# A hedgehog linear-attention layer and a GEGLU FFN on one core: an eight-bank PSUM pool, and phi_q@KV two tiles at a time

## The chip, the core and the metric

The kernel runs on one NeuronCore of a Trainium2 chip. TensorE multiplies matrices into PSUM (eight banks of 128 partitions by 512 fp32). VectorE and ScalarE read PSUM, do the elementwise work and write SBUF; GpSimd works from SBUF alone; SyncE issues the DMAs. The engines run side by side and wait for each other through semaphores. The metric is the device time of one execution in microseconds.

## The reference

A sequence of 2048 rows of width 640, bf16. First the attention layer on the layer-normed input, 32 heads of width 20, then the FFN on the layer-normed sum:

```
q, k, v = layernorm(x) @ wqkv                       # 2048 x 640 each, 32 heads of 20
phi(a)  = [softmax(a @ w_phi), softmax(-a @ w_phi)]  # per head: 20 + 20 features
kv      = phi(k)^T @ v ; z = sum_s phi(k)            # per head: 40 x 20 and 40
o       = phi(q) @ kv / (phi(q) @ z + 1e-6)
h       = x + o @ wo
out     = h + (gelu(layernorm(h) @ w_gate) * (layernorm(h) @ w_up)) @ w_down   # inner width 1536
```

## The kernel before

The rows are 16 tiles of 128, in four blocks of four tiles. The first part (up to about 90 us) makes the normed input, transposed, in four SBUF tiles LN1T0 to LN1T3; from it k, v and q. It accumulates phi(k)^T v over all 16 tiles in one PSUM tile and masks it into KV (line 352). Exp of q and of -q stay in SBUF, transposed, as Eq (line 367), unnormalised: since the positive and the negative features have their own denominators, the products for each sign s are kept apart.

From line 490 on, PSUM is one pool `psG` of four slots of two banks; every PSUM tile (`gtile`, line 100) takes one. The framework picks the slot and makes the next writer wait until all readers of the slot's former tile have finished. Where a tile has two banks, a reader of one bank waits, as the trace shows, for the products of both.

A tile t of attention output goes through these steps, each a function of its own:

- `attn_a` (522): phi_q@KV. Twenty matmuls of 64 contraction rows by 88 columns, those of the upper and the lower 64 rows (u = 0, 1) into two PSUM tiles `ab`, so that both half-arrays work at once; for each sign s one bank of each. Then two copies of 128x704 fp32 into an SBUF tile AB. In the main part both are ScalarE's; for tiles 0 and 1 one, for tile 2 both are VectorE's.
- `attn_b`, `attn_b2`, `attn_b3` (526 to 558): denominators and weights on GpSimd (`pr`, `den`, `w`), a reciprocal `rd` on VectorE, and on VectorE the weighted numerators `tt` and their sum `o`. Then a DMA transposes o into oT.
- `attn_c` (565): o @ wo, ten matmuls into a two-bank tile `po`.
- `attn_d` (574), `attn_d2` (587): VectorE adds po to x_sb and sums the row on the way; ScalarE sums the squares; five GpSimd ops make the scale and shift of the second layer norm.
- `attn_e` (604): ScalarE applies them (ln), a DMA transposes into LN2T of the tile's block.

The FFN has two kinds of units. `gate_up(b, f, a0, a1)` (610) makes 128 of the 1536 inner features for the columns a0 to a1 of block b: five gate matmuls in one bank, five up matmuls in the other bank of one tile `gu`; Gelu on ScalarE reads the first, a product on VectorE (GT) reads the second and ends the tile's life. `down(b, tl, u)` (623) makes half u (320 columns) of an output tile: twelve matmuls into one bank of `pd`; after both halves VectorE adds x_sb to all 640 columns in one instruction (y, line 641), and a store follows later.

The order of work is written out by hand: a manual schedule fixes each engine's instructions in program order. `weave(units, stages)` (657) walks through a list of units, and before unit i it emits every stage whose number is at most i; what is left goes over to the next weave. `attn_at(t, i, offs)` gives tile t's steps the numbers i + offset.

- Before the weaves: tiles 0 and 1 run between the last q products; then `attn_e(1)` (a transpose on TensorE and a VectorE copy into LN2T), then `attn_a(2, 2)`.
- Weave 1 has 16 units: block 0, columns 0 to 256, twelve gate/up units (0 to 11), then four downs (12 to 15) for its tiles 0 and 1. Beside it run tiles 2 to 6.
- Weave 2 is the same for columns 256 to 512 and tiles 2 and 3, with tile 7 and what is left.
- Then blocks 1 to 3, twelve 512-wide gate/up units and eight downs each. Beside block b run the four tiles of block b + 1.

So `attn_a` comes 14 times in the weaves or just ahead of them, one tile at a time, between units.

Of the kernel before, what the change touches and what calls it, by code (L numbers as in the profile page):

```python
# [8 lines left out]
BF16 = mybir.dt.bfloat16  # L9
F32 = mybir.dt.float32  # L10
ALU = mybir.AluOpType
ACTF = mybir.ActivationFunctionType
AX = mybir.AxisListType
PSUM = bass.MemoryType.PSUM
# [3 lines left out]
def kernel(  # L18
# [12 lines left out]
    nc = tc.nc  # L31
    P = 128
    S = 2048
    D = 640
    H = 32
# [3 lines left out]
    NB = NT // 4  # L39
    NC = D // P  # L40
    NF = FF // P
    EPS = 1e-5
    HD = D // 2
# [15 lines left out]
    KC = Dh + 2  # L59


    UH = H // 2
# [3 lines left out]
    o_v = out.rearrange("b (p t) d -> p (b t) d", t=NT)  # L66
# [25 lines left out]
    def eq(t, c, s):  # L92
        for E, g in zip(Eq, QG):
            if t // 4 * NC + c in g:
                return E[:, g.index(t // 4 * NC + c), s, t % 4 * P:(t % 4 + 1) * P]

    def small(pool, shape, name, bufs=3):
        return pool.tile(shape, F32, name=name, bufs=bufs)

    def gtile(name):  # L100
        return psG.tile([P, 2, 512], F32, name=name, tag="G")
# [49 lines left out]


    mid = ctx.enter_context(tc.tile_pool(name="mid", bufs=1, side="right"))
    LN1T = [mid.tile([P, NC, 512], BF16, name=f"LN1T{b}") for b in range(NB)]
    Wq2 = mid.tile([P, NC, D], BF16, name="Wq2")
    p1_cm = tc.tile_pool(name="p1", bufs=1, reuse_waits="tile")
    p1 = p1_cm.__enter__()
# [329 lines left out]
    ev_cm.__exit__(None, None, None)  # L487
    p1_cm.__exit__(None, None, None)
    ps_cm.close()
    psG = ctx.enter_context(tc.tile_pool(name="psG2", bufs=4, space=PSUM, reuse_waits="tile"))  # L490


    p2 = ctx.enter_context(tc.tile_pool(name="p2", bufs=1, reuse_waits="tile"))
# [1 line left out]
    Wd = p2r.tile([P, NF, D], BF16, name="Wd")  # L495
    nc.sync.dma_start(Wd, B_w_down.rearrange("(c p) n -> p c n", p=P))

    LN2T, st = {}, {}

    def attn_a_mm(t):  # L500

        b = t // 4
        if b not in LN2T:
            LN2T[b] = p2.tile([P, NC, 512], BF16, name="LN2T", bufs=2)
        AB = p2r.tile([P, 2, H, KC], F32, name="AB", bufs=2)
        ab = gtile("ab"), gtile("ab")
        for s in range(2):
            for c in range(NC):
                for u, r in enumerate(HALF):
                    nc.tensor.matmul(ab[u][:, s, 3 * c * KC:(3 * c + 4) * KC], lhsT=eq(t, c, s)[r],  # L510
                                     rhs=KV[r, c, s].rearrange("p h f -> p (h f)"),
                                     start=(c == 0), stop=(c == NC - 1), skip_group_check=True)
        st[t] = AB, ab

    def attn_a_ev(t, dve=0):
        AB, ab = st[t]
        for u in range(2):
            (nc.vector.tensor_copy if u >= 2 - dve else nc.scalar.copy)(  # L518
                AB[:, :, u * UH:(u + 1) * UH].rearrange("p s h f -> p s (h f)"), ab[u][:, :, 0:UH * KC])
        st[t] = AB  # L520

    def attn_a(t, dve=0):
        attn_a_mm(t)
        attn_a_ev(t, dve)

    def attn_b(t, on_pe=False):

# [36 lines left out]

    def attn_c(t):

        po = gtile("po")
        for u in range(2):
            for c in range(NC):
                nc.tensor.matmul(po[:, u, 0:HD], lhsT=st[t][:, c, :], rhs=Wo[:, c, u * HD:(u + 1) * HD],  # L570
                                 start=(c == 0), stop=(c == NC - 1))
        st[t] = po

    def attn_d(t, act=True):

        ht = x_sb[t // 4][:, t % 4, :]
        h2 = ht.rearrange("p (u f) -> p u f", u=2)
        if not act:
            nc.vector.tensor_tensor(h2, st[t][:, :, 0:HD], h2, ALU.add)
            st[t] = ln_stats(p2, [ht], "2", False)[0]  # L580
            return

        sm = small(p2, [P, 2], "sm", 2)
        nc.vector.scalar_tensor_tensor(h2, st[t][:, :, 0:HD], 1.0, h2, op0=ALU.mult, op1=ALU.add, accum_out=sm[:, 0:1])
        st[t] = sm

    def attn_d2(t):
        sm = st[t]
        ht = x_sb[t // 4][:, t % 4, :]
        sq = p2.tile([P, D], BF16, name="sq", bufs=1)  # L590
        nc.scalar.activation(sq, ht, ACTF.Square, accum_out=sm[:, 1:2])
        v = small(p2, [P, 3], "v2", 2)
        nc.gpsimd.tensor_scalar(v[:, 0:1], sm[:, 0:1], sm[:, 0:1], -1.0 / (D * D), op0=ALU.mult, op1=ALU.mult)
        nc.gpsimd.tensor_scalar_add(v[:, 0:1], v[:, 0:1], EPS)
        nc.gpsimd.tensor_scalar(v[:, 1:2], sm[:, 1:2], 1.0 / D, v[:, 0:1], op0=ALU.mult, op1=ALU.add)
        rstd = small(p2, [P, 1], "rstd2")
        nc.gpsimd.tensor_tensor(rstd, v[:, 1:2], nhalf[:, 0:1], op=ALU.pow)
        nc.gpsimd.tensor_scalar(v[:, 2:3], sm[:, 0:1], rstd, -1.0 / D, op0=ALU.mult, op1=ALU.mult)  # L598
        st[t] = ht, None, rstd, v[:, 2:3]
# [8 lines left out]
        transpose_to(LN2T[t // 4][:, :, t % 4 * P:(t % 4 + 1) * P], ln, on_pe, on_dve)  # L608

    def gate_up(b, f, a0, a1):  # L610
        gu = gtile("gu")
        n = a1 - a0
        for i, W in ((0, Wg), (1, Wu)):
            for c in range(NC):
                nc.tensor.matmul(gu[:, i, 0:n], lhsT=W[:, c, f * P:(f + 1) * P], rhs=LN2T[b][:, c, a0:a1],  # L615
                                 start=(c == 0), stop=(c == NC - 1))
        g = p2.tile([P, 512], BF16, name="g", bufs=3)
        nc.scalar.activation(g[:, 0:n], gu[:, 0, 0:n], ACTF.Gelu_apprx_tanh)  # L618
        if (b, "g", f) not in st:
            st[b, "g", f] = p2.tile([P, 512], BF16, name="GT", bufs=NF + 2)  # L620
        nc.vector.tensor_tensor(st[b, "g", f][:, a0:a1], gu[:, 1, 0:n], g[:, 0:n], ALU.mult)  # L621

    def down(b, tl, u):
        if u == 0:
            st["pd"] = gtile("pd"), p2.tile([P, D], BF16, name="y", bufs=4)
        pd, y = st["pd"]
        if u == 1 and b == NB - 1 and tl == 3:
            pd = gtile("pd")
        last = b == NB - 1 and tl == 3

        cuts = [(0, 192), (192, HD)] if last and u == 1 else [(0, HD)]
        for n0, n1 in cuts:
            if n0:
                pd = gtile("pd")
            for f in range(NF):
                nc.tensor.matmul(pd[:, u, n0:n1], lhsT=st[b, "g", f][:, tl * P:(tl + 1) * P],  # L636
                                 rhs=Wd[:, f, u * HD + n0:u * HD + n1], start=(f == 0), stop=(f == NF - 1))
            if u == 1 or last:
                a = u if last else 0
                r = lambda x: x.rearrange("p (u f) -> p u f", u=2)[:, a:u + 1, n0:n1]  # L640
                nc.vector.tensor_tensor(r(y), pd[:, a:u + 1, n0:n1], r(x_sb[b][:, tl, :]), ALU.add)  # L641
                f0, f1 = a * HD + n0, u * HD + n1
                stores.append((lag, o_v[:, 4 * b + tl, f0:f1], y[:, f0:f1]))
                if b == NB - 1 and tl >= 2:
                    store(lag)

# [10 lines left out]
    def weave(units, stages):  # L657

        stages = sorted(later + stages, key=lambda x: x[0])
        later.clear()  # L660
        for i, (fn, *args) in enumerate(units):
            while stages and stages[0][0] <= i:
                _, g, *a = stages.pop(0)
                g(*a)
            store(1)
            fn(*args)
        later.extend((i - len(units), g, *a) for i, g, *a in stages)

    def gus(b, a0, a1):
        return [(gate_up, b, f, a0, a1) for f in range(NF)]  # L670

    def downs(b, tls):
        return [(down, b, tl, u) for tl in tls for u in range(2)]


    q_mm(q)
    attn_a(0, 1)
    q_exp(q)
    q_mm(q + 1)
    attn_b(0, True)  # L680
    attn_b2(0, True)
    attn_b3(0, True)
    attn_a(1, 1)
    q_exp(q + 1)
    q_mm(q + 2)
    attn_t(0)
# [21 lines left out]
        q_exp(j)  # L708
    attn_ln(1, True)
    attn_e(1, True, True)  # L710
    attn_a(2, 2)
    assert q + 9 == len(Eq)

    def attn_at(t, i, offs):

        fns = (attn_a, attn_b, attn_b2, attn_b3, attn_c, attn_d, attn_d2, attn_e)
        return [(i + o, fn, t) for fn, o in zip(fns, offs) if o >= 0]

    SHORT = (0, 2, 3, 4, 9, 9, 10, 12)
    SHORT2 = (0, 2, 3, 4, 10, 10, 11, 13)  # L720
    LONG = (0, 1, 2, 3, 6, 6, 7, 8)


    weave(gus(0, 0, 256) + downs(0, (0, 1)),
          attn_at(2, 0, (-1, 0, 1, 2, 7, 7, 8, 10)) + attn_at(3, 1, SHORT) + attn_at(4, 6, SHORT2) + attn_at(5, 9, SHORT2) +
          attn_at(6, 13, SHORT2))
    weave(gus(0, 256, 512) + downs(0, (2, 3)), attn_at(7, 0, SHORT))
    for b in range(1, NB):
        stages = []
        if b + 1 < NB:  # L730
            for tl in range(4):
                stages += attn_at(4 * b + 4 + tl, (0, 2, 5, 7)[tl], LONG)
        weave(gus(b, 0, 512) + downs(b, range(4)), stages)
    man_cm.__exit__(None, None, None)


# [28 lines left out]
```

## Time and profile before

| | us |
|---|---|
| median of three runs (278.71 to 279.73) | 279.65 |
| span of the profiled execution, first to last instruction | 277.2 |
| outside that span (median less span) | 2.45 |
| TensorE busy | 271.6 (98%) |
| VectorE busy | 167.3 (60%) |
| ScalarE busy | 143.5 (52%) |
| GpSimd busy | 94.7 (34%) |
| first gate product starts at | 90.88 |
| block 0 of the FFN ends, block 1 begins | about 141.4 |
| granted TensorE clock, all of the span | 1.0 |

The profiler lists instructions with start and duration on one core; PE is TensorE, DVE VectorE, ACT ScalarE, POOL GpSimd. Matmuls are pipelined: a matmul's duration is longer than its distance to the next one. In a timeline line the columns are start, time from the first start to the last end, engine, line, operation, output and inputs, shapes, count, and in brackets the idle time before it with what ended it. The chain that ended last is followed back from the last instruction; its columns are start, time, engine, what, count. VectorE is busiest early: its busy share is nine tenths and more in the slices up to 76 us, some six tenths between 91 and 141 us (31.25 of 50.40), and a half in blocks 1 and 2 (46.50 of 93.90).

### The profile page before, as it was taken

To read this page: it belongs to the slowest core of one execution; us is meant where nothing else is said; L and a number is where in the kernel's file an instruction comes from. 1 tells how busy PE (TensorE), PEld (TensorE's weight loads), DVE (VectorE), ACT (ScalarE), POOL (GpSimd) and SP (SyncE) were. 2 spreads that over 40 slices of the span, in tenths; PEclk is the share of its full clock that TensorE was granted. 3 is DMA by queue.
4 is the path that set the end of the run, shared out by engine and by line. 5 is a ranking of instruction groups with operands and counts; after the bars stand their busy time and mean duration, and the time that the engine had idled before them with its cause. 6 is when DMAs were issued, how large, how long until landed. Compare 5 with 4: busy or idle time off the path is not lost.

```text
span 277.2 us, 5817 instructions
## 1 busy us (share of the span) xinstructions
PE 271.6 (98%) x2337; PEld 172.1 (62%) x2337; DVE 167.3 (60%) x292; ACT 143.5 (52%) x239; POOL 94.7 (34%) x213
## 2 busy tenths in 40 slices
PE   7899999999999999999999999999999999999995
PEld 3677777764555887788754555675455567444574
DVE  6799999899496776675325757322666622233222
ACT  4879998778598755374524364413445440222200
POOL 4348997765202217365301353400226230000000
PEclk9999999999999999999999999999999999999999
DMA  7965732489730021324120213130022413000011
GB/s 204 192 232 112 99 74 47 44 256 393 255 102 0 4 47 36 85 49 77 30 65 2 47 27 63 32 88 33 14 36 25 73 25 95 26 0 0 0 50 47
DMA packets 42235, 21.37 MB, mean 77 GB/s; under 512 B 35040, under 2 KB 40416, under 8 KB 42208
## 3 DMA queue, kind: packets, MB, share of 16 engines
q1 hardware_dynamic: 42208, 21.01, 30.8%
q8 instruction: 18, 0.29, 0.5%
q14 instruction: 9, 0.07, 0.1%
HBM read 10.18 MB, written 2.62 MB: 46 GB/s over the span
## 4 chain that ended last, share of the span: by engine, by line
PE 87%; SPq 3%; DMA 3%; DVE 2%; ACT 2%; issue 1%
PE gu L615 38%; PE pd L636 19%; PE pq L362 8%; PE po L570 8%; PE pk L274 5%; PE pv L274 4%; PE ab L510 3%; PE kvp L340 2%; SPq L186 2%; DMA LN1T<-ln 2%; DVE stats L110 1%; DMA WkT<-in_A_wqkv_dram 1%; ACT E L307 1%; ACT ln L134 1%; PE wa L228 1%
## 5 line engine op out<-in xcount | busy, mean ns | idle before, releaser
L621 DVE TENSOR_TENSOR GT<-gu,g 128x512 bf16<-128x512 f32 (+1 forms) x60 | 34.4, 580 | 54.3 <-ACT g L618 54.1
L618 ACT ACTIVATE g<-gu 128x512 bf16<-128x512 f32 (+1 forms) x60 | 30.7, 512 | 69.3 <-PE gu L615 68.5
L615 PE MATMUL gu<-LN2T,Wg 128*128 128x512 bf16 (+1 forms) x300 | 61.9, 337 | 0.1
L615 PE MATMUL gu<-LN2T,Wu 128*128 128x512 bf16 (+1 forms) x300 | 61.8, 337 | 0.0
L636 PE MATMUL pd<-Wd,GT 128*128 128x320 bf16 (+2 forms) x396 | 53.8, 295 | 0.0
L636 PEld LDWEIGHTS <-GT 128*128 128x128 bf16 x396 | 37.9, 98 | 15.3 <-DVE GT L621 0.9
L615 PEld LDWEIGHTS <-Wu 128*128 128x128 bf16 x300 | 29.3, 98 | 22.6
L615 PEld LDWEIGHTS <-Wg 128*128 128x128 bf16 x300 | 28.3, 98 | 20.8
L274 PEld LDWEIGHTS <-LN1T 128*128 128x128 bf16 x290 | 27.9, 98 | 11.0 <-DMA LN1T<-ln 0.3
L322 POOL TENSOR_TENSOR vt<-vS,rs 128x672 bf16<-128x672 bf16 x22 | 29.1, 1344 | 9.1 <-DVE rs L318 7.4
L641 DVE TENSOR_TENSOR y<-pd,x_sb 128x640 bf16<-128x640 f32 (+3 forms) x18 | 13.5, 749 | 30.2 <-PE pd L636 30.2
L518 ACT COPY AB<-ab 128x704 f32<-128x704 f32 x28 | 19.6, 748 | 19.8 <-PE ab L510 19.6
L551 DVE TENSOR_TENSOR tt<-AB,w 128x1280 bf16<-128x1280 f32 x16 | 23.8, 1486 | 1.0 <-POOL w L544 0.9
L570 PE MATMUL po<-Wo,oT 128*128 128x320 bf16 x160 | 24.3, 299 | 0.0
L274 PE MATMUL pk<-Wk,LN1T 128*128 128x320 bf16 x160 | 24.0, 299 | 0.0
L314 DVE TENSOR_REDUCE sk<-E 128x64 f32<-128x1280 bf16 x16 | 22.9, 1434 | 1.2 <-ACT E L307 1.2
L362 PE MATMUL pq<-LN1T,Wq 128*128 128x512 bf16 x100 | 22.9, 379 | 0.0
L367 ACT ACTIVATE Eq<-pq 128x1024 bf16<-128x1024 f32 (+1 forms) x26 | 19.9, 830 | 2.4 <-PE pq L362 2.4
L307 ACT ACTIVATE E<-pk 128x640 bf16<-128x640 f32 x28 | 18.3, 716 | 4.5 <-PE pk L274 4.3
L570 PEld LDWEIGHTS <-oT 128*128 128x128 bf16 x160 | 15.6, 98 | 7.0 <-ACT oT L148 0.3
L274 PE MATMUL pv<-Wv,LN1T 128*128 128x320 bf16 x130 | 19.8, 299 | 0.2 <-DMA LN1T<-ln 0.2
L134 ACT ACTIVATE ln<-x_sb,v,rstd 128x640 bf16<-128x640 bf16 x14 | 12.9, 919 | 11.3 <-POOL v L598 11.1
(101 smaller groups left out, 268.1 us busy)
## 6 DMA issues: line engine op xcount, KB each, us to landing
out_dram<-y SPq DMA_DIRECT2D x15, 160.0 KB, 1.8
Wg<-in_B_w_gate_dram SPq DMA_DIRECT2D x1, 1920.0 KB, 9.4
Wu<-in_B_w_up_dram SPq DMA_DIRECT2D x1, 1920.0 KB, 15.3
Wd<-in_B_w_down_dram SPq DMA_DIRECT2D x1, 1920.0 KB, 7.9
x_sb<-in_A_x_dram SPq DMA_DIRECT2D x2, 640.0 KB, 5.5
Wo<-in_A_wo_dram SPq DMA_DIRECT2D x1, 800.0 KB, 11.1
x_sb<-in_A_x_dram SPq DMA_DIRECT2D x4, 160.0 KB, 3.1
Wv<-in_A_wqkv_dram SPq DMA_DIRECT2D x2, 320.0 KB, 4.1
```

The lines of the kernel that those rows point to most:

```text
L274: nc.tensor.matmul(ps[:, u, 0:HD], lhsT=lnT(t, c), rhs=W[:, c, u * HD:(u + 1) * HD], start=(c == 0), stop=(c == NC - 1))
L307: nc.scalar.activation(Ek[t][:, s, :].rearrange("p (u f) -> p u f", u=2), pk[:, :, 0:HD], ACTF.Exp, scale=((lnp[t][2], nrstd[t]) if t in C ...
L314: nc.vector.reduce_sum(sk, Ek[t].rearrange("p s (h f) -> p (s h) f", f=Dh), axis=AX.X)
L322: eng.tensor_tensor(vt[:, s], vS[t % 8], rs[:, s * H:(s + 1) * H, None].to_broadcast([P, H, VC]), ALU.mult)
L362: nc.tensor.matmul(pqs[j][:, i, :], lhsT=Wq2[:, kc, c * P:(c + 1) * P], rhs=LN1T[b][:, kc, :], start=(kc == 0), stop=(kc == NC - 1))
L367: nc.scalar.activation(Eq[j][:, :, s, :], pqs[j][:, 0:len(QG[j])], ACTF.Exp, scale=(1.0, -1.0)[s])
L551: nc.vector.tensor_tensor(tt.rearrange("p s (h f) -> p s h f", f=Dh), num, w[:, :, :, None].to_broadcast([P, 2, H, Dh]), ALU.mult)
L570: nc.tensor.matmul(po[:, u, 0:HD], lhsT=st[t][:, c, :], rhs=Wo[:, c, u * HD:(u + 1) * HD], start=(c == 0), stop=(c == NC - 1))
L615: nc.tensor.matmul(gu[:, i, 0:n], lhsT=W[:, c, f * P:(f + 1) * P], rhs=LN2T[b][:, c, a0:a1], start=(c == 0), stop=(c == NC - 1))
L618: nc.scalar.activation(g[:, 0:n], gu[:, 0, 0:n], ACTF.Gelu_apprx_tanh)
L621: nc.vector.tensor_tensor(st[b, "g", f][:, a0:a1], gu[:, 1, 0:n], g[:, 0:n], ALU.mult)
L636: nc.tensor.matmul(pd[:, u, n0:n1], lhsT=st[b, "g", f][:, tl * P:(tl + 1) * P], rhs=Wd[:, f, u * HD + n0:u * HD + n1], start=(f == 0), sto ...
```

## The change

From the start of the FFN part, PSUM is a pool `psB` of eight slots of one bank. Gate and up products have a bank each; each half of a down has one and its own VectorE add of 320 columns; po of tiles 2 and up has two banks, with an add and a row sum per bank, and a GpSimd instruction to add the two sums.

`attn_pair(t)` does phi_q@KV of tiles t and t + 1 back to back, forty matmuls into eight banks, and then issues the copies, one for each bank (128x352): the banks of u = 0 on ScalarE, those of u = 1 on VectorE. It is called seven times, for tiles 2, 4, ... 14; the single calls for tiles 3, 4, 5, 6 and 7 stood ahead of units 1, 6, 9 and 13 of weave 1 and unit 0 of weave 2. Pair (2, 3) stands where `attn_a(2, 2)` stood, in the new pool. Pair (4, 5) stands ahead of unit 6 of weave 1, pair (6, 7) ahead of unit 14, pair (8, 9) ahead of unit 14 of weave 2, pair (10, 11) ahead of block 1's first unit, pair (12, 13) ahead of block 1's unit 18 and pair (14, 15) ahead of block 2's first. Five AB tiles are in use instead of two; three of them lie in the memory of LN1T, which therefore becomes one SBUF tile seen in two types. The numbers of the later steps are set anew. In weave 1: tile 2's b3 2, c 7 and e 10; tile 3's b3 at 5 and c at 10 as before; tile 4's b3 at 10; tile 5's b3 at 12 instead of 13. Tile 7's b, b2, b3 and c fall to units 2, 3, 4 and 9 of weave 2.

```diff
-    LN1T = [mid.tile([P, NC, 512], BF16, name=f"LN1T{b}") for b in range(NB)]
+    LN1F = mid.tile([P, NB * NC * 256], F32, name="LN1T")
+    LN1T = [LN1F.bitcast(BF16).rearrange("p (b c n) -> p b c n", b=NB, c=NC)[:, b] for b in range(NB)]
...
+    ABs = [p2r.tile([P, 2, H, KC], F32, name=f"AB{i}") for i in range(2)]
+    ABs += [LN1F[:, i * 2 * H * KC:(i + 1) * 2 * H * KC].rearrange("p (s h f) -> p s h f", s=2, h=H) for i in range(3)]
+    def bank(name):
+        return psB.tile([P, 512], F32, name=name, tag="B")
...
+    def attn_pair(t):
+        for i in (t, t + 1):
+            ab = [[None] * 2, [None] * 2]
+            for s in range(2):
+                for u in range(2):
+                    ab[u][s] = bank("ab")
+            attn_a_mm(i, ab)
+            st[i] = ab
+        for i in (t, t + 1):
+            AB = ABs[i % len(ABs)]
+            for s in range(2):
+                for u, eng in enumerate((nc.scalar.copy, nc.vector.tensor_copy)):
+                    eng(AB[:, s, u * UH:(u + 1) * UH].rearrange("p h f -> p (h f)"), st[i][u][s][:, 0:UH * KC])
+            st[i] = AB
...
-        nc.vector.scalar_tensor_tensor(h2, st[t][:, :, 0:HD], 1.0, h2, op0=ALU.mult, op1=ALU.add, accum_out=sm[:, 0:1])
+        for u in range(2):
+            nc.vector.scalar_tensor_tensor(h2[:, u], st[t][u], 1.0, h2[:, u], op0=ALU.mult, op1=ALU.add,
+                                           accum_out=sm[:, u:u + 1])
...
+        nc.gpsimd.tensor_tensor(sm[:, 0:1], sm[:, 0:1], sm[:, 1:2], ALU.add)
...
-        gu = gtile("gu")
+        gu = bank("gu"), bank("gu")
...
-            if u == 1 or last:
-                nc.vector.tensor_tensor(r(y), pd[:, a:u + 1, n0:n1], r(x_sb[b][:, tl, :]), ALU.add)
+            pd = bank("pd")[:, 0:n1 - n0]
...
+            nc.vector.tensor_tensor(y[:, f0:f1], pd, x_sb[b][:, tl, f0:f1], ALU.add)
...
-    attn_a(2, 2)
+    psB = ctx.enter_context(tc.tile_pool(name="psB", bufs=8, space=PSUM, reuse_waits="tile"))
+    attn_pair(2)
...
+    EARLY = (0, 1, 2, 7, 7, 8, 10)
+    SHORT = (0, 1, 2, 8, 8, 9, 11)
+    LONG = (0, 1, 2, 5, 5, 6, 7)
     weave(gus(0, 0, 256) + downs(0, (0, 1)),
+          attn_at(2, 0, EARLY) + attn_at(3, 3, EARLY) + [(6, attn_pair, 4)] + attn_at(4, 8, SHORT) + attn_at(5, 10, SHORT) +
+          [(14, attn_pair, 6)] + attn_at(6, 15, SHORT) + attn_at(7, 18, EARLY))
+    weave(gus(0, 256, 512) + downs(0, (2, 3)),
+          [(14, attn_pair, 8), (16, attn_pair, 10)] + attn_at(8, 15, LONG) + attn_at(9, 17, LONG) + attn_at(10, 19, LONG) +
+          attn_at(11, 21, LONG))
+    weave(gus(1, 0, 512) + downs(1, range(4)),
+          [(18, attn_pair, 12), (20, attn_pair, 14)] + attn_at(12, 19, LONG) + attn_at(13, 21, LONG) +
+          attn_at(14, 23, LONG) + attn_at(15, 25, LONG))
+    for b in (2, 3):
+        weave(gus(b, 0, 512) + downs(b, range(4)), [])
```

## The prediction

> **What bounds the kernel now.** I read the page's busy times first, then the chain that ended last (in order of time), then the timelines of VectorE, ScalarE and TensorE around the attention products, then the waits.
>
> ```profile
> PE 271.6 (98%) x2337; PEld 172.1 (62%) x2337; DVE 167.3 (60%) x292; ACT 143.5 (52%) x239; POOL 94.7 (34%) x213
> ```
> ```profile
> 90.34 0.50 DVE LN2T L148
> ...
> 90.88 1.25 PE gu L615 x10
> ...
> 188.35 0.50 PE ab L510 x20
> 188.85 4.42 PE gu L615 x20
> ...
> 235.24 25.90 PE gu L615 x120
> ```
> From 32.9 us to the end this chain is TensorE, apart from one 0.5 us eviction at 90.34. In the last block 120 products take 25.90 us, 0.216 each. So whatever TensorE loses or saves after 90 us reaches the end at full price; work of the other engines counts only where TensorE waits for it. The span is 277.2 us, the median 279.65, so 2.45 us lie around the span; I add my sum to the median. About 0.5% (1.4 us) is what a measurement can tell from no change.
>
> ```profile
> 188.28 0.57 PE L510 MATMUL ab<-KV,Eq 64*128 64x88 bf16 x20
> ```
> This TensorE timeline line is one tile's phi_q@KV, "a visit". 0.57 us run from the first start to the last end; one matmul takes 0.20 (its group's mean is 204 ns), so the ten steps (two half-arrays start together) are 0.37/9, or 0.04 us, apart: 0.40 us of streaming. On the chain the visit costs 0.50, and the 20 products behind it take 4.42 instead of 20 x 0.216 = 4.32. So 0.60 per visit, 0.20 of it for going to half-array form and back.
>
> **What the merging saves.** Tiles 0 and 1 are untouched. Of tiles 2 to 15, tile 2's visit (90.23) lies under the LN2T copy that the first gate product waits for, and is free now. Thirteen visits are on the chain: 13 x 0.60 = 7.8 us. Afterwards six pairs cost 2 x 0.40 + 0.20 = 1.00 each: 6.0. The first pair (tiles 2, 3) runs before the FFN, and its eight banks are all of PSUM, so one of them is the bank that the last Exp reads:
>
> ```profile
> 89.47 1.67 ACT L367 ACTIVATE Eq<-pq 128x512 bf16<-128x512 f32 x3
> 91.16 1.28 ACT L618 ACT_TABLE_LOAD   x1
> 92.45 0.38 ACT L618 ACTIVATE g<-gu 128x256 bf16<-128x256 f32 x1
> ```
> That Exp ends at 91.14, and a waiting matmul follows 0.05 later (copy ended 90.83, gate product 90.88). If this bank comes last in the pair, 0.2 of streaming and 0.1 of switch remain: gates start at 91.5, 0.6 later than now. If it comes first: 91.19 + 0.8 + 0.1 = 92.1, 1.2 later. The profile does not show the order of banks; I take +1.0, as most orders block early. Together: -7.8 + 6.0 + 1.0 = -0.8 us (ends -1.2 and -0.6).
>
> The Trainium skill's "TensorEngine Tiling (Array Packing)", Key Properties, says that changing the tiling mode drains TensorE, which is the 0.20 above. Its section on the PSUM bottleneck speaks against this change: tiling speeds up TensorE but not PSUM evacuation. By the first rule alone the sum would end here, at -0.8 us; by the second the waits worked out next come on top, +3.2 in all.
>
> **What the pair waits for.** The copies are issued after both tiles' products, so a pair holds eight banks at once. Its last bank must be the one released last by the work ahead. Today's pool has four units of slack: VectorE may be 2.5 us late and nobody notices. At a pair the slack is gone, except for the 0.1 + 0.6 us until the last quarter is touched.
>
> Pair (4, 5) stands ahead of unit 6, behind six 256-wide gate/up units. VectorE there, today:
>
> ```profile
> 92.87 0.42 DVE L621 TENSOR_TENSOR GT<-gu,g 128x256 bf16<-128x256 f32 x1 [0.35 <-ACT g L618]
> ...
> 94.44 0.42 DVE L621 TENSOR_TENSOR GT<-gu,g 128x256 bf16<-128x256 f32 x1 [0.78 <-ACT g L618]
> 94.78 1.48 DVE L551 TENSOR_TENSOR tt<-AB,w 128x1280 bf16<-128x1280 f32 x1
> ...
> 98.31 1.49 DVE L551 TENSOR_TENSOR tt<-AB,w 128x1280 bf16<-128x1280 f32 x1 [0.32 <-POOL w L544]
> 99.83 0.49 DVE L555 TENSOR_TENSOR o<-tt 128x640 bf16<-128x640 bf16 x1
> 100.24 0.75 DVE L621 TENSOR_TENSOR GT<-gu,g 128x256 bf16<-128x256 f32 x2
> ```
> The sixth GT (unit 5) is the first of the two at 100.24 and ends at 100.66, though its products were done at about 98.2: it is queued behind tile 3's tt and o. The new order keeps that queue (both b3 steps stand ahead of the same units). From the first GT to the end of the sixth is 7.8 us; the 0.78 wait shrinks to about 0.3, as ScalarE has no copies left there: 7.3. The first GT moves: the pair's four ScalarE half-copies now stand between the last Exp and the table load. Gelu at 512 and at 256 elements takes 597 and 383 ns, 0.84 ns an element; a copy of 352 instead of 704 (748 ns) then takes about 450 ns, and some 350 when it follows another (two of 704 together take 1.39 us); four of them, the first ready at about 91.6, end at about 93.0. Load to 94.3, Gelu to 94.7, GT from 94.7, sixth GT done at 102.0. TensorE: gates at 91.9, six units of 1.09, switch 0.1, three quarters 0.6: it wants that bank at 99.1. Stall 2.9. If the load stays ahead of the copies, the first Gelu is set by its products (92.7), GT at 93.1, the sixth done at 100.4: stall 1.2. I take 2.5, nearer the upper end, because the instruction order says so.
>
> Pair (6, 7) stands behind both downs of tile 0. Today those end at 110.82 + 1.63 = 112.45, but the y add runs from 114.35 to 115.16, 2.7 us late, behind tile 5's tt (112.36) and o. If that lateness stays, the pair stalls 2.7 - 0.7 = 2.0; tile 5's b3 now comes one unit (1.63) earlier, which leaves about 0.4, and the add is two of 0.49 in place of one of 0.82. I take 1.0 (0 to 2.0).
>
> Pairs 8 to 14 stand among downs, where VectorE only adds:
>
> ```profile
> 272.68 0.49 DVE L641 TENSOR_TENSOR y<-pd,x_sb 128x320 bf16<-128x320 f32 x1 [0.81 <-PE pd L636]
> ```
> That add starts some 0.2 behind its last product's slot and frees the bank at 0.2 + 0.49 + 0.05 = 0.74, against 0.7: 0.05 each, 0.2 for four (0 to 0.8).
>
> Tile 7's attention chain in the second half of block 0 has the least cover. Today its o ends at 126.32, the transpose lands 2.6 us later (the median of these issues) at 128.9, and its po product starts at 130.15: 1.2 us to spare. The steps from b3 to c stay five units apart. But its b2 step moves behind tile 5's d2 in GpSimd's order (both now fall to the same unit, tile 5 first; today d2 comes a unit later). Today d2 is five small GpSimd ops (with a Square on ScalarE between), which hold its queue for 2.2 us after the po add (tile 6: 130.29 to 132.51); then it is six, 2.5 us. w, and with it VectorE's tt, can be that much later. I take 0.3 us of waiting at po (0 to 1.3: nothing if d2 ends before rd is ready, or 2.5 less the 1.2).
>
> **Costed at nothing.** Splits: the y adds grow by 2 x 0.49 - 0.82 = 0.16 per tile, the po adds by that and a second accumulator read (0.08); VectorE waits 30.2 us for pd in today's run, which covers them outside block 0. Half the AB copies go from ScalarE (748 ns for 704) to VectorE (886; about 0.52 per half, half of 886 and of the 0.16 that a split costs); tile 2's already were there. GpSimd's added 128x1 sum, some 0.27 by the den rows (266 ns), delays each LN2T transpose by that; tile 7's is issued four downs (6.5 us) ahead of its reader, and lands in 2.6. If that cover is gone it costs 0.27 once per block. Gelu waits today for both banks (it starts 0.03 behind the up products); it can now start one bank earlier, which is in my Gelu times. Putting LN1T into one tile costs nothing as long as reuse is tracked by range; the gate products read one half of LN2T unbroken while transposes write the other half.
>
> **Sum.** -0.8 + 2.5 + 1.0 + 0.2 + 0.3 = +3.2 us: 279.65 + 3.2 = 282.85, said as 282.8. The ends add to -1.2 + 1.2 = 0.0 and -0.6 + 2.9 + 2.0 + 0.8 + 1.3 = +6.4, 279.6 to 286.0; all upper ends at once are unlikely.
>
> **Rivals.** (a) VectorE keeps up, and the merging is all that is seen: 279.65 - 0.8 = 278.9, at best 278.4. Place: the sixth GT. It decides if that GT ends by 99.2, and the y add ahead of pair (6, 7) within 0.7. For it speaks the earlier Gelu; against it the 4.0 us of tt and o plus six GTs in line before the bank is freed. This is the not-slower side: no change, 0.13; with one of the switches saved beyond it, faster.
> (b) The lateness spreads: two stalls shift VectorE and GpSimd against each other in block 0, GpSimd's ops stretch beside tt (today v at L593 takes 1436 ns at 107.46 against 264 at rest), oT and LN2T come late, and po products or the last f of a down wait too. A further 1 to 3 us over the sum, 284 to 286: 0.16. Against it: today tiles 4 and 5 have 3.7 us between oT landing and po (tile 4: 111.95 to 115.65).
> (c) The shared LN1T ties transposes in the first stage to readers of other blocks. TensorE has hardly a gap from 33 to 90 us, so any such wait shows: 3 us or more, from 286 on, 0.05. Against it: LN2T above.
> (d) The switch is paid per tile all the same, because a wait falls between the two tiles of a pair: the 7 x 0.20 are lost, +1.2 on the sum, within the range.
>
> **Chances.** Forecast with (d) 0.66, (a) 0.13, (b) 0.16, (c) 0.05. Faster by over 0.5% (below 278.25) needs (a) and more than its best end less 0.15: 0.06. Within 0.5% (to 281.05) takes the rest of (a) and the low end of the forecast: 0.18. Slower 0.76. The range runs from 279.0, just above (a)'s middle, to 285.4, well into (b), and leaves out about 0.2.
>
> **What would show it.** Right: ab in seven runs of 40 with the clock at 1.0; in the pair ahead of unit 6, TensorE idle 2 to 3 us with VectorE GT as releaser, after ten or more ab products; about 1 us at the pair behind tile 0's downs with y as releaser; the first gate product at 91.5 to 92.1; TensorE's waits absent from 140 us on. Wrong: pairs of 1.0 us without a break (rival a), or breaks at po, pd and gu instead of at ab (rival b), or any new gap before 90 us (rival c). The prediction fails most easily in VectorE's lateness at unit 6, since 2.5 of the 3.2 us hang on it.

## The result, and the profile after

The changed kernel takes 283.17 us (median; 282.83 to 284.55) against 279.65 before: a ratio of 1.0148, 95% interval 1.0122 to 1.0174. The profiled execution has a span of 281.5 us with 1.67 around it. For the kernel before, median less span gives 2.45, but other executions of it have about 1.7 around their span (278.98 us against 277.3), so that median and that span are most likely of different executions.

The busy times of the page of after, by engine:

```profile
PE 271.3 (96%) x2324; PEld 173.4 (62%) x2337; DVE 180.9 (64%) x361; ACT 136.9 (49%) x241; POOL 97.3 (35%) x227
```

TensorE is busy for 0.3 us less than before (13 records of matmuls are missing here), in a span 4.3 us longer. The added time is waiting. The chain that ended last (start, length, what), which before was TensorE's from 91 us on, now goes through VectorE, GpSimd and a DMA as well:

```profile
93.72 2.17 issue
...
96.44 1.65 DVE tt L567
...
109.92 1.41 POOL sm L615
...
114.08 1.50 DVE tt L567
...
132.72 2.58 DMA oT<-o
...
265.49 13.08 PE pd L657 x108
```

All but the last of these lie in block 0; behind the DMA it is TensorE's again to the last matmul, apart from pieces of "issue" of 0.05 us ("issue" is time for which the profile shows no cause). TensorE's waits, in its timeline of after, around the first three pairs and at tile 7's po. Each line is a run of matmuls: start, length, then in brackets the idle time ahead of the run and its releaser:

```profile
91.23 1.25 PE L515 MATMUL ab<-KV,Eq 64*128 64x88 bf16 x40 [0.58 <-DVE LN2T L148]
...
99.07 0.60 PE L515 MATMUL ab<-KV,Eq 64*128 64x88 bf16 x21
99.86 0.55 PE L515 MATMUL ab<-KV,Eq 64*128 64x88 bf16 x19 [0.19 <-DVE GT L644]
...
102.53 1.52 PE L590 MATMUL po<-Wo,oT 128*128 128x320 bf16 x10 [0.92 <-DVE GT L644]
...
112.72 1.94 PE L657 MATMUL pd<-Wd,GT 128*128 128x320 bf16 x13 [0.23 <-DVE GT L644]
114.59 0.76 PE L515 MATMUL ab<-KV,Eq 64*128 64x88 bf16 x30
116.55 0.20 PE L515 MATMUL ab<-KV,Eq 64*128 64x88 bf16 x1 [1.20 <-DVE y L659]
116.95 0.35 PE L515 MATMUL ab<-KV,Eq 64*128 64x88 bf16 x9 [0.20 <-DVE y L659]
...
135.35 1.53 PE L590 MATMUL po<-Wo,oT 128*128 128x320 bf16 x10 [0.78 <-DMA oT<-o]
```

The bracket holds idle time only. Below, a "break" is the distance from one matmul's start to the next, less the usual distance for that kind, which also takes in restarting; it is up to 0.2 us more than the bracket.

How to compare two kernels here matters. The time at which the last transpose ahead of the FFN starts lies between 89.73 and 90.72 us in the profiles of the changed kernel and its variants, though nothing ahead of it differs between them. That noise is as large as some of the effects. So I measure the **stretch** from that transpose to the last matmul's start. It is 184.00 us before and 187.91 after: +3.91. Each stretch is read from one profiled execution. The timed ratio gives 1.48% of 279.65, or +4.1.

The parts that can be read from the two traces: from the last transpose to the first gate product 0.80 us before and 1.99 after, +1.19. Break in pair (4, 5) 0.38, at tile 2's po 1.06, in tile 0's downs 0.13 and 0.40, in pair (6, 7) 1.76, at tile 7's po 0.93, at the four late pairs 0.06 each, 0.24: 4.90 together. The merged visits at the working's own prices (6 x 1.00 in place of 13 x 0.60) give -1.8. The sum is 1.19 + 4.90 - 1.8 = +4.29, 0.38 above the 3.91 measured. Of that, 0.25 are three steps of 0.08 in the later downs of the kernel before (at 175.28, 222.16 and 262.55 us), which the changed kernel does not have; the last 0.13 stay open.

### The profile page after: what moved, and what is told of

Same layout as the page of the kernel before. It is cut to its first block, busy times and chain, and to the rows that moved or that the text cites. A ratio compares the mean times of both kernels' runs of the same rounds, so it can differ in the third digit from the quotient of the medians.

```text
span 281.5 us, 5954 instructions
## 1 busy us (share of the span) xinstructions
PE 271.3 (96%) x2324; PEld 173.4 (62%) x2337; DVE 180.9 (64%) x361; ACT 136.9 (49%) x241; POOL 97.3 (35%) x227
## 4 chain that ended last, share of the span: by engine, by line
PE 83%; DVE 4%; SPq 3%; POOL 3%; issue 2%; DMA 2%; ACT 1%; POOLq 0%; DVEq 0%
PE gu L638 32%; PE pd L657 18%; PE pk L275 8%; PE pq L363 7%; PE po L590 7%; PE pv L275 6%; PE kvp L341 2%; PE ab L515 2%; SPq L187 2%; DVE tt L567 2%; DMA WkT<-in_A_wqkv_dram 1%; DMA oT<-o 1%; PE wa L229 1%; DVE LN1T L539 1%; POOL w L560 1%
## 5 line engine op out<-in xcount | busy, mean ns | idle before, releaser
L641 ACT ACTIVATE g<-gu 128x512 bf16<-128x512 f32 (+1 forms) x60 | 30.2, 509 | 77.2 <-PE gu L638 74.6
L638 PEld LDWEIGHTS <-Wg 128*128 128x128 bf16 x300 | 29.0, 98 | 21.3
L659 DVE TENSOR_TENSOR y<-pd,x_sb 128x320 bf16<-128x320 f32 (+2 forms) x33 | 15.8, 481 | 31.0 <-PE pd L657 31.0
L363 PEld LDWEIGHTS <-Wq 128*128 128x128 bf16 x100 | 9.5, 98 | 10.4 <-issue 0.2
L539 ACT COPY LN1T<-ab 128x352 f32<-128x352 f32 x18 | 7.1, 464 | 15.9 <-PE ab L515 15.8
```

What stands on the lines that cost most here:

```text
L363: nc.tensor.matmul(pqs[j][:, i, :], lhsT=Wq2[:, kc, c * P:(c + 1) * P], rhs=LN1T[b][:, kc, :], start=(kc == 0), stop=(kc == NC - 1))
L638: nc.tensor.matmul(gu[i][:, 0:n], lhsT=W[:, c, f * P:(f + 1) * P], rhs=LN2T[b][:, c, a0:a1], start=(c == 0), stop=(c == NC - 1))
L641: nc.scalar.activation(g[:, 0:n], gu[0][:, 0:n], ACTF.Gelu_apprx_tanh)
L659: nc.vector.tensor_tensor(y[:, f0:f1], pd, x_sb[b][:, tl, f0:f1], ALU.add)
```

## The experiments

Each edit is to the changed kernel unless said otherwise. Each ratio is to the kernel before. My theory: four separate places lose the time (the first pair; the sixth GT behind tile 3's b3 step; the y adds of tile 0 behind tile 5's b3; tile 7's b2 behind tile 5's d2 on GpSimd), each by the order of instructions on an engine other than TensorE. Its rivals: the split adds and copies make VectorE too slow for any order; or a wait that is removed only comes up at the next consumer.

**The first pair split.** Tile 2 goes back ahead of the change of pools, tile 3 stands alone at unit 1 of the FFN.

```diff
+    attn_a(2)
     ps_cm.close()
...
-    attn_pair(2)
...
-          attn_at(2, 0, EARLY) + attn_at(3, 3, EARLY) + [(6, attn_pair, 4)] + attn_at(4, 8, SHORT) + attn_at(5, 10, SHORT) +
+          attn_at(2, 0, EARLY) + [(1, attn_one, 3)] + attn_at(3, 3, EARLY) + [(6, attn_pair, 4)] + attn_at(4, 8, SHORT) + attn_at(5, 10, SHORT) +
```

The new `attn_one` is the pair's body for one tile: four banks, the products, four half copies.

> The changed kernel, but tile 2's phi_q@KV runs alone in the old two-bank pool ahead of the FFN, under the LN2T copy, and tile 3's alone ahead of unit 1 in the new pool. Theory (the first pair waits 0.36 us for the last Exp's bank and puts 40 matmuls ahead of the first gate product): from the last transpose's start to the first gate product 0.8 us as in the old kernel instead of 1.99 in the changed one, and one visit of 0.60 more at unit 1: about 0.6 us faster than the changed kernel (282.6). Rival (the first gate product waits for the new pool, whoever comes before it): the 1.99 stays and the time is 0.6 us above the changed kernel's.

Measured: 281.88 us, ratio 1.0073 (1.0044 to 1.0102); stretch 187.01, 0.90 less than the change. In TensorE's timeline of this kernel:

```profile
89.51 0.44 PE L147 MATMUL tp<-ident,ln 128*128 128x128 bf16 x5
89.89 0.57 PE L515 MATMUL ab<-KV,Eq 64*128 64x88 bf16 x20
90.53 0.71 PE L651 MATMUL gu<-LN2T,Wg 128*128 128x256 bf16 x5
```

The products of tile 2 lie straight behind the transposes, and the first gate follows without a wait for Exp or LN2T beyond the old 0.80. By the rows: 1.19 gained here, 0.60 paid for tile 3's lone visit, and a smaller break at tile 2's po, 0.80 in place of 1.06: 0.85, against 0.90 measured. Pair (4, 5) breaks at other products than before, but takes as long, 1.47 us from the product ahead of it to the one behind it in both.

**Tile 3's b3 step one unit later**, so that the sixth GT is issued to VectorE ahead of tile 3's tt and o.

```diff
-          attn_at(2, 0, EARLY) + attn_at(3, 3, EARLY) + [(6, attn_pair, 4)] + attn_at(4, 8, SHORT) + attn_at(5, 10, SHORT) +
+          attn_at(2, 0, EARLY) + attn_at(3, 3, (0, 1, 3, 7, 7, 8, 10)) + [(6, attn_pair, 4)] + attn_at(4, 8, SHORT) + attn_at(5, 10, SHORT) +
```

> The changed kernel with one number moved: tile 3's tt and o come behind unit 5's GT on VectorE instead of ahead of it. Theory (tile 2's po takes the bank that this GT frees, and waits 1.06 us for it because tt and o stand in front): GT ends about 2 us earlier, the gap ahead of tile 2's po goes from 1.06 to under 0.1 us, the pair's own break of 0.39 stays (it hangs on unit 4's GT); 1.0 us faster, about 282.1. Rival (the pool is short because the pair's eight banks are not copied yet): the gap ahead of po stays or grows, as the pair's VectorE copies now come 2 us later; time the same or up to 1 us slower.

Measured: 282.95 us, 1.0122 (1.0081 to 1.0164); stretch 187.58, only 0.33 less. TensorE of this kernel:

```profile
101.04 0.71 PE L638 MATMUL gu<-LN2T,Wu 128*128 128x256 bf16 x5
101.58 1.52 PE L590 MATMUL po<-Wo,oT 128*128 128x320 bf16 x10
...
111.87 0.31 PE L657 MATMUL pd<-Wd,GT 128*128 128x320 bf16 x1 [0.59 <-DVE GT L644]
112.41 1.80 PE L657 MATMUL pd<-Wd,GT 128*128 128x320 bf16 x12 [0.23 <-DVE GT L644]
```

The wait at tile 2's po is gone, as expected: the sixth GT was its cause. But the first of the two breaks in tile 0's downs, which need the GTs of the last two units, has grown from 0.13 to 0.75. VectorE of after, and then of this kernel (their last transposes are 0.01 apart):

```profile
100.12 1.49 DVE L567 TENSOR_TENSOR tt<-LN1T,w 128x1280 bf16<-128x1280 f32 x1 [0.32 <-POOL w L560]
...
102.06 0.42 DVE L644 TENSOR_TENSOR GT<-gu,g 128x256 bf16<-128x256 f32 x1
...
104.44 0.49 DVE L605 SCALAR_TENSOR_TENSOR x_sb<-po,x_sb 128x320 bf16<-128x320 f32 x1
```
```profile
99.45 0.69 DVE L644 TENSOR_TENSOR GT<-gu,g 128x256 bf16<-128x256 f32 x2
...
104.13 0.48 DVE L605 SCALAR_TENSOR_TENSOR x_sb<-po,x_sb 128x320 bf16<-128x320 f32 x1
...
108.05 0.35 DVE L556 RECIPROCAL rd<-den 128x32 f32<-128x32 f32 x1 [1.42 <-POOL den L549]
```

The sixth GT went into the 0.32 us for which VectorE had stood waiting for tile 3's w. Everything behind it on VectorE (tt, o, the pair's copies, tile 2's po add, the last two GTs) comes 0.31 earlier and no more, while TensorE, freed of 1.06, asks for those GTs earlier than that. Of the 1.06, 0.62 come back in the downs and 0.13 in a step inside pair (4, 5). VectorE's queue gave them back. Part of that queue is idle time: 1.42 us ahead of tile 4's reciprocal, the same in both kernels (at 108.36 in the changed one), because GpSimd works on tile 2's d2 before it makes tile 4's den.

**Tile 5's b3 step behind the y adds of tile 0.**

```diff
-          attn_at(2, 0, EARLY) + attn_at(3, 3, EARLY) + [(6, attn_pair, 4)] + attn_at(4, 8, SHORT) + attn_at(5, 10, SHORT) +
+          attn_at(2, 0, EARLY) + attn_at(3, 3, EARLY) + [(6, attn_pair, 4)] + attn_at(4, 8, SHORT) + attn_at(5, 10, (0, 1, 4, 8, 8, 9, 11)) +
```

> The changed kernel with one number moved: tile 5's tt and o come behind the two y adds of tile 0, ahead of pair (6, 7), instead of ahead of the adds. Theory (pair (6, 7) waits for the banks that these adds free): its break goes from 1.76 us to about 0.1, 1.6 us faster, about 281.5; the 0.54 us break inside tile 0's downs stays, since it hangs on a GT. Rival (the break is set by the pair's need for eight banks while po and gu hold theirs): break stays over 1 us, time within 0.5 us of the changed kernel.

Measured: 281.42 us, 1.0065 (1.004 to 1.0091); stretch 186.19, 1.72 less. VectorE of after, and then TensorE and VectorE of this kernel:

```profile
114.08 1.49 DVE L567 TENSOR_TENSOR tt<-AB,w 128x1280 bf16<-128x1280 f32 x1 [1.41 <-POOL w L560]
115.60 0.49 DVE L571 TENSOR_TENSOR o<-tt 128x640 bf16<-128x640 bf16 x1
116.02 0.88 DVE L659 TENSOR_TENSOR y<-pd,x_sb 128x320 bf16<-128x320 f32 x2
```
```profile
114.54 1.00 PE L515 MATMUL ab<-KV,Eq 64*128 64x88 bf16 x40
```
```profile
114.65 0.49 DVE L659 TENSOR_TENSOR y<-pd,x_sb 128x320 bf16<-128x320 f32 x1 [1.14 <-PE pd L657]
115.05 1.48 DVE L567 TENSOR_TENSOR tt<-AB,w 128x1280 bf16<-128x1280 f32 x1
```

The two y adds no longer stand behind tt and o (and behind the 1.41 that tt waits for GpSimd's w), and the pair runs as one piece of 40 matmuls in 1.00 us. The 1.76 was this queue.

**Tile 5's d2 (and e) step one unit later**, behind tile 7's b2 on GpSimd.

```diff
-          attn_at(2, 0, EARLY) + attn_at(3, 3, EARLY) + [(6, attn_pair, 4)] + attn_at(4, 8, SHORT) + attn_at(5, 10, SHORT) +
+          attn_at(2, 0, EARLY) + attn_at(3, 3, EARLY) + [(6, attn_pair, 4)] + attn_at(4, 8, SHORT) + attn_at(5, 10, (0, 1, 2, 8, 8, 10, 12)) +
```

> The changed kernel with one number moved: tile 5's d2 (six GpSimd ops) comes a unit later, so that tile 7's w no longer queues behind it on GpSimd. Theory: tile 7's oT lands 1 to 2 us earlier and the 0.92 us wait ahead of its po goes; 0.9 us faster, about 282.2. Rival (VectorE, not GpSimd, sets tile 7's tt): the wait stays within 0.3 us of 0.92 and the time is the same.

Measured: 282.41 us, 1.0093 (1.0064 to 1.0121); stretch 186.96, 0.95 less. TensorE of this kernel at tile 7's po, which waited 0.93 for oT:

```profile
134.16 0.71 PE L638 MATMUL gu<-LN2T,Wu 128*128 128x256 bf16 x5
134.71 1.52 PE L590 MATMUL po<-Wo,oT 128*128 128x320 bf16 x10
```

The wait is gone, and its whole size is gained.

**All four together** (tile 5 at `(0, 1, 4, 8, 8, 10, 12)`).

> The four edits of the first series together (tile 2 alone in the old pool, tile 3's and tile 5's tt and o behind the GT and the adds, tile 5's d2 a unit later). Theory (the breaks are separate late releases, so that what each edit took out adds up): 0.9 + 0.35 + 1.76 + 0.94 = 3.95 us off the changed kernel, 279.2, level with the old one; the breaks left are the pair ahead of unit 6 (0.2 to 0.4) and tile 0's downs (0.4 + 0.75). Rival (breaks only move on to the next shortage of banks): a new break of over 0.5 us appears elsewhere and the time stays above 280.5.

Measured: 279.63 us, 1.0005 (0.9989 to 1.0022); stretch 184.05. The four gains add to 0.90 + 0.33 + 1.72 + 0.95 = 3.90, and together they give 3.86: the four edits do not interfere. What is left, in TensorE's timeline of this kernel:

```profile
110.44 0.31 PE L670 MATMUL pd<-Wd,GT 128*128 128x320 bf16 x1 [0.61 <-DVE GT L657]
110.97 1.94 PE L670 MATMUL pd<-Wd,GT 128*128 128x320 bf16 x13 [0.23 <-DVE GT L657]
```

These are the breaks that the second experiment had left, 0.77 + 0.40 here.

**GpSimd's order too.** On top of the last: tile 2's d2 (and e) goes behind tile 4's den, and tile 5's b2 one unit later, behind tile 3's d2.

```diff
-          attn_at(2, 0, EARLY) + [(1, attn_one, 3)] + attn_at(3, 3, (0, 1, 3, 7, 7, 8, 10)) + [(6, attn_pair, 4)] + attn_at(4, 8, SHORT) + attn_at(5, 10, (0, 1, 4, 8, 8, 10, 12)) +
+          attn_at(2, 0, (0, 1, 2, 7, 7, 10, 12)) + [(1, attn_one, 3)] + attn_at(3, 3, (0, 1, 3, 7, 7, 8, 10)) + [(6, attn_pair, 4)] + attn_at(4, 8, SHORT) + attn_at(5, 10, (0, 2, 4, 8, 8, 10, 12)) +
```

> As the run before it, and tile 2's d2 and tile 5's b2 later, so that on GpSimd tile 4's pr, den and w no longer queue behind d2. Theory (VectorE idles 1.4 us ahead of tile 4's rd because den stands behind tile 2's d2 on GpSimd, and this makes the last two GTs late for tile 0's downs): rd 1.4 us earlier, both breaks in the downs gone, 1.1 us less than the run before it: about 278.1, 0.5% under the old kernel. Rival (the adds of po and tile 4's tt alone fill VectorE there): the downs keep breaks of 0.5 us or more and the time stays within 0.5 us of the run before it.

Measured: **278.42 us (277.84 to 279.39), ratio 0.9972 (0.9957 to 0.9988)**; stretch 183.11, 0.94 less again. VectorE and TensorE of this kernel:

```profile
104.64 0.34 DVE L569 RECIPROCAL rd<-den 128x32 f32<-128x32 f32 x1
```
```profile
108.66 3.42 PE L670 MATMUL pd<-Wd,GT 128*128 128x320 bf16 x24
...
113.20 3.42 PE L670 MATMUL pd<-Wd,GT 128*128 128x320 bf16 x24 [0.18 <-ACT AB L539]
```

Tile 4's reciprocal no longer waits for GpSimd, and tile 0's downs run unbroken. A break of 0.25 is new behind pair (6, 7), where the next down waits for a ScalarE copy. The interval of the ratio lies below 1: this version is ahead of the kernel before, though by 0.28% only, less than the 0.5% that I had called measurable.

**Pairs only where VectorE has time, and no pairs at all.** Two kernels keep the one-bank pool and all split adds and copies, and put block 0's tiles back as single visits at the numbers they had before (tile 2 in the old pool). One keeps the pairs of tiles 8 to 15; the other has none.

```diff
-          attn_at(2, 0, EARLY) + attn_at(3, 3, EARLY) + [(6, attn_pair, 4)] + attn_at(4, 8, SHORT) + attn_at(5, 10, SHORT) +
-          [(14, attn_pair, 6)] + attn_at(6, 15, SHORT) + attn_at(7, 18, EARLY))
+          attn_at1(2, 0, (-1, 0, 1, 2, 7, 7, 8, 10)) + attn_at1(3, 1, SHORT1) + attn_at1(4, 6, SHORT2) +
+          attn_at1(5, 9, SHORT2) + attn_at1(6, 13, SHORT2))
```

> The one-bank pool, block 0 with single tiles at the old kernel's numbers (tile 2 in the old pool), pairs for tiles 8 to 15 alone. Theory: no break in block 0 but what VectorE's split instructions add; four switches of 0.2 us saved, four times 0.06 us waited: 0.6 us under the run after it, and about 279.1, 0.2% under the old kernel. Rival (a pair costs as much in waits as it saves anywhere): level with the run after it.

> The one-bank pool and the adds and copies per bank, but every tile's phi_q@KV alone at the old kernel's numbers. Theory (the pool is free of charge, the pairs and the new numbers in block 0 cost): within 0.5 us of the old kernel, 279.3 to 280.2, thirteen visits of 0.60 on TensorE and no break of over 0.3 us. Rival (the splits make VectorE late): breaks in block 0 of 1 us and more without any pair, 281 or more.

Measured: with the late pairs 279.4 us, 1.0003 (0.999 to 1.0016), stretch 184.28. Without any pair 280.17, 1.0037 (1.002 to 1.0054), stretch 184.94. The difference, 0.66, is what four late pairs save: 0.165 each, the 0.20 for a switch less some 0.04 to 0.06 of waiting. Behind block 0 neither trace has another wait on TensorE, so for these four pairs the merging does what was said.

The second reading was not expected. The pool of one-bank slots with its splits and copies, and no pair, costs 0.94 in the stretch against the kernel before. Its breaks are 0.74 and 0.20 in tile 0's downs and 0.27 at a po. VectorE of this kernel, and below it the two GTs that answer in the kernel before (both traces have their last transpose at 90.07 to 90.08, so the times compare directly):

```profile
106.26 0.35 DVE L569 RECIPROCAL rd<-den 128x32 f32<-128x32 f32 x1 [1.43 <-POOL den L562]
106.53 0.89 DVE L552 COPY AB<-ab 128x352 f32<-128x352 f32 x2
...
110.41 0.75 DVE L657 TENSOR_TENSOR GT<-gu,g 128x256 bf16<-128x256 f32 x2
```
```profile
109.20 0.75 DVE L621 TENSOR_TENSOR GT<-gu,g 128x256 bf16<-128x256 f32 x2
```

GT comes 1.2 us later. The two half copies in front of it, 0.89, were ScalarE's before. But the reciprocal ahead of them is late already, by 0.64 (105.62 in the kernel before), and another difference has a part in this. Both copies of tile 2 were VectorE's; now one is ScalarE's, ahead of the load of the Gelu table. ScalarE of the kernel without pairs:

```profile
91.02 0.75 ACT L524 COPY LN1T<-ab 128x704 f32<-128x704 f32 x1
91.79 1.28 ACT L654 ACT_TABLE_LOAD   x1
```

In the kernel before the load starts at 91.16, and so the first GT comes 0.64 later here (93.50 against 92.87). No run takes this copy back, so its share of the 0.94 stays open.

**Whose are these 0.94?** Two runs give the copies back to ScalarE: in the kernel without pairs (tiles 3 and up), and in the fastest kernel (tiles 3 to 7).

```diff
         for s in range(2):
-            for u, eng in enumerate((nc.scalar.copy, nc.vector.tensor_copy)):
-                eng(AB[:, s, u * UH:(u + 1) * UH].rearrange("p h f -> p (h f)"), ab[u][s][:, 0:UH * KC])
+            for u in range(2):
+                nc.scalar.copy(AB[:, s, u * UH:(u + 1) * UH].rearrange("p h f -> p (h f)"), ab[u][s][:, 0:UH * KC])
```

> The kernel without pairs of the last series, with the single tiles' copies all on ScalarE, as in the old kernel. Theory (the 0.9 us of breaks in tile 0's downs without any pair come from the copies that moved to VectorE, 0.9 us ahead of the last two GTs, and from the split po adds): the breaks there shrink from 0.94 to 0.3 us or less, the stretch from the last transpose to the last matmul from 184.9 to about 184.2, level with the old kernel's 184.0. Rival (the one-bank pool itself is short there): the breaks stay.

> The kernel with the reordered GpSimd and VectorE steps (278.4), and the copies of tiles 3 to 7 all on ScalarE. Theory (VectorE sets block 0, ScalarE has room): its two breaks of 0.14 and 0.27 us go, 0.2 to 0.4 us less. Rival (four to eight copies in a row on ScalarE hold the Gelu and the pair's banks): a break of 0.3 us or more behind the pairs, time the same or above 278.6.

Measured, without pairs: 279.54 us, 1.001 (0.9997 to 1.0022), stretch 184.87. The breaks in the downs are gone. Counted from the last transpose, the last two GTs end at 20.30 us in place of 21.09, so the copies on VectorE made most of those breaks; what was left does not show, since TensorE reaches the downs 0.47 later. But the stretch is only 0.07 shorter: new breaks stand at two po products, 0.75 and 0.39. The first, in TensorE's timeline, and what ScalarE and VectorE did ahead of it:

```profile
98.93 0.71 PE L651 MATMUL gu<-LN2T,Wu 128*128 128x256 bf16 x5
100.22 0.99 PE L603 MATMUL po<-Wo,oT 128*128 128x320 bf16 x6 [0.59 <-DMA oT<-o]
```
```profile
93.12 1.52 ACT L552 COPY LN1T<-ab 128x352 f32<-128x352 f32 x4
```
```profile
94.96 0.42 DVE L657 TENSOR_TENSOR GT<-gu,g 128x256 bf16<-128x256 f32 x1 [1.02 <-ACT g L654]
95.30 1.48 DVE L580 TENSOR_TENSOR tt<-LN1T,w 128x1280 bf16<-128x1280 f32 x1
```

Tile 2's oT lands late here. Tile 3's four half copies in a row hold ScalarE for 1.52 us, the next Gelu comes behind them, a GT waits 1.02 for it, and tile 2's tt stands behind that GT. That this chain is what delays oT I argue from the rows; no run isolates it. In the fastest kernel, copies on ScalarE give 278.91 us, 0.9974 (0.9961 to 0.9988), stretch 183.28: 0.17 longer, no gain. In this order it does not matter which of the two engines copies.

Pairs in the old pool of two-bank slots, and the shared LN1T alone, were not tried.

## Why the prediction was right or wrong

The forecast was 282.8 us and the result is 283.17. The sum, +3.2 against +3.5 by the medians and +3.9 by the stretch, is near partly by luck: its terms were off in opposite directions, one by -1.1, others by +1.3, +0.6 and +0.2.

**What bounds it: right.** Every break of TensorE after 90 us appeared in the time, and each one removed was gained (3.86 of 3.90), unless another wait took its place.

**The merging, -0.8 with the first pair at +1.0: right in mechanism and nearly in size.** Four late pairs save 0.66 where the working gives 4 x (0.20 - 0.05) = 0.6. The first gate came 1.19 later; undoing this pair gave 0.90. The wait named for the first pair, the last Exp, is joined by the LN2T copy, as the 0.58 in its line says.

**Pair (4, 5), 2.5 us: the step failed.** "A pair holds eight banks at once. Its last bank must be the one released last by the work ahead." The pair never held eight, and it did not need the sixth GT's bank: its last product ends at 100.41, two us before that GT does, and the 0.19 in its line is a wait for the fifth GT, which ends at 99.80. In the program's list of banks the pair's eighth tile takes the bank of its own first tile, which a ScalarE copy frees while TensorE is still at the pair. The ab tile's rows in the trace show these copies:

```profile
L539 ACT COPY LN1T<-ab x2: 452/455/458, 99.5 to 99.8; 128x352 f32<-128x352 f32 x2
```

The first runs from 99.5 to 99.9, inside the pair (99.07 to 100.41). In the same list the bank of the sixth GT goes to tile 2's po. The sixth GT itself was where I had put it: it starts at 102.06 and takes 0.42 in VectorE's timeline, 102.48 against the 102.0 worked out. But TensorE could do the rest of the pair and one more unit before it needed that bank. The wait moved to po and shrank, 0.38 + 1.06 = 1.44 in place of 2.5. The second experiment shows the GT as the cause of the po wait. I had written that breaks at po would speak for rival (b); here a break at po has the forecast's own cause at another place.

**Pair (6, 7), 1.0: right in mechanism, mis-sized.** It measured 1.76, with 0.13 and 0.40 more in the downs ahead of it. The working counted tt and o in front of the y adds but took a unit's earlier start of b3 at full value. On the chip tt waited 1.41 for GpSimd's w, which follows tile 3's d2 in that queue (the last section has its rows). Moving the step before it helps nothing while the operand comes later. Putting b3 behind the y adds gained 1.72.

**Tile 7's po, 0.3: right in place and cause, mis-sized** within its ends (0 to 1.3): 0.93, and exactly the queue on GpSimd that was named, as moving d2 gained 0.95.

**Late pairs, 0.05 each: right** (0.06).

**Costed at nothing: the splits and copies failed in block 0.** The cover I named, VectorE's 30.2 us of waiting for pd, lies outside block 0, as the text itself said; inside it nothing was priced. With no pair at all this part costs 0.94 us, together with tile 2's copy ahead of the table load. In the changed kernel it cannot be separated from the breaks already counted, since it acts through the same GTs. That is why the places' sum still came out nearly.

**Rivals.** (a), VectorE keeps up, fell: four places broke. (b) came in part, as 0.53 in the downs and the larger waits at (6, 7) and tile 7, without reaching its 284. (c) is not seen: the last transposes lie at 89.73 to 90.72 in eleven traces with the shared LN1T, against 90.08 before. (d) is not what happened: the unbroken pairs ran as 40 matmuls in 1.00 us.

The Trainium skill's "TensorEngine Tiling (Array Packing)", on the PSUM bottleneck, says that packing speeds up TensorE and not the evacuation. The runs agree as far as block 0 goes (4.7 us of breaks against 1.8 us of visits taken off the chain). They add that this was a matter of order: with the first pair split again and five steps in other places, the same evacuation kept up, and the kernel was 0.28% faster than before.

## What to carry to other kernels

A saving on the engine that bounds the kernel counts only where the engines that release its buffers are on time; before tightening a pool, list for each engine what stands in its queue ahead of each releasing instruction, GpSimd's queue included. A buffer that is late does not stall the user you look at but the one that the pool hands it to, so follow the buffer and not the program's order. Where a removed wait brings less than its size, see how much earlier the engine that releases the buffers now runs: in the second experiment TensorE was freed of 1.06 us and VectorE came 0.31 earlier, and 0.33 was gained. And measure from a fixed event near the change, since the part ahead of it can vary by more than the effect.

## What the runs showed of the hardware

Splitting costs about the same on both engines, some 0.06 us for each instruction more. On ScalarE one copy of 352 columns takes 0.45 us, and four in a row take 1.52, against 1.39 for two of 704: 0.13 for two more. On VectorE the split add of 320 columns takes 0.49 alone, and two in a row take 0.88 (y at 116.02), against 0.82 for one of 640: 0.06 for one more. The working had put it at 0.16, from twice 0.49; two in a row overlap in the profile.

The sum that the split adds on GpSimd was put at 0.27 us. In GpSimd's timeline of after it is once less than that and once five times as much:

```profile
105.42 0.19 POOL L615 TENSOR_TENSOR sm<-sm 128x1 f32<-128x1 f32 x1 [5.34 <-DVE x_sb L605]
...
109.88 1.44 POOL L615 TENSOR_TENSOR sm<-sm 128x1 f32<-128x1 f32 x1
...
113.56 0.48 POOL L560 TENSOR_TENSOR w<-AB,rd 128x32 f32<-128x32 f32 x2
```

The second one lies within VectorE's tt (109.72, 1.55 us) and ends 0.05 us behind it; beside the first, VectorE runs a GT. It is on the chain shown above with 1.41 us, and the w for which tile 5's tt waits 1.41 is at the end of this d2. The stretch is not new, however. In the kernel before, the first operation of the same d2, another one, lies beside the same tt (107.27, 1.49 us) and is stretched as much:

```profile
107.45 1.44 POOL L593 TENSOR_SCALAR v<-sm 128x1 f32<-128x1 f32 x1 [0.92 <-DVE x_sb L584]
```

So it goes with the place beside tt and not with the operation. The whole d2 takes 3.72 us after (109.88 to 113.60) and 3.29 before (107.45 to 110.74): with the added operation of one column this step is 0.43 us longer, where 0.27 were put down.
